# Polynomial-sketch attention followed by a ReGLU FFN: shared PSUM banks, attention released evenly over FFN units, and finer TensorE and ScalarE pieces

## The chip, the cores and the metric

The kernel runs on one core of one Trainium2 chip. The metric is the device time of one execution in microseconds (us). Before the change the median of three runs is 133.13 us (132.45 to 133.69). Five engines work beside each other, each through a queue of its own in order: TensorE (PE; its weight loads are listed as PEld), VectorE (DVE), ScalarE (ACT), GpSimd (POOL) and SyncE (SP, which here only issues DMAs). The PSUM memory, into which TensorE writes, has eight banks of 128 x 512 fp32.

## The reference

```python
def _attn_ref(q, k, v, S1, S2):             # q, k, v: (4, 4, 1088, 32); S1, S2: (8, 32)
    def phi(x):
        a = np.einsum('rd,bhsd->bhsr', S1, x)
        b = np.einsum('rd,bhsd->bhsr', S2, x)
        return np.einsum('bhsi,bhsj->bhsij', a, b).reshape(*x.shape[:-1], r * r)
    q_p, k_p = (phi(q), phi(k))
    kv = np.einsum('bhsf,bhsd->bhfd', k_p, v)
    z = np.sum(k_p, axis=2)
    num = np.einsum('bhsf,bhfd->bhsd', q_p, kv)
    den = np.einsum('bhsf,bhf->bhs', q_p, z)[..., None] + 1e-06
    return (num / den).astype(np.float32)

def _moe_ref(x, w_gate, w_val, w_out):      # x: (4352, 128), d_ff = 1536
    gate = np.maximum(x @ w_gate, 0.0)
    val = x @ w_val
    return (gate * val @ w_out).astype(np.float32)
```

The attention output, with its heads side by side, is the FFN's `x`: 4 batches x 1088 positions, 128 channels. All inputs and the output are fp32 in device memory.

## The kernel before

**The FFN.** It is cut into 102 units, in the order of ten groups of positions. A group is a pair of a batch and a first block of 128 positions. Batch 0 has three groups, of 256, 256 and 512 positions (units 0 to 5, 6 to 11 and 12 to 23). Batches 1 to 3 have two groups of 512 positions each, 12 units a group. The last group, of 256, holds the 64 last positions of all four batches (units 96 to 101). A unit takes 128 hidden channels for 512 positions, or 256 channels for 256 positions. Its steps are `gate` (L458, TensorE into a PSUM bank), `relu` (L464, ScalarE, PSUM to `g_sb`), `val` (L470, TensorE), `prod` (L475, VectorE, `g_sb` times the PSUM of `val`, into `ht`) and `out` (L485, four TensorE products that accumulate into the group's output bank over the group's units). After the last unit of a group, `store` (L493) copies the output bank to `o_sb` on ScalarE and SyncE sends it out (L496).

**Attention, keys.** Class `K` does one batch: `t1` transposes the keys (L249, VectorE, `kt`), `ab` multiplies them by the sketches in fp32 (L257, TensorE), `t2` transposes back (L267, `abk`), `phi` forms the outer products (L205, `kp`, mostly GpSimd), `kv` (L283) and `kv_rest` (L295) multiply by the values, `z` (L308) and `z_rest` (L318) sum the features in fp32, `zdiag` (L324) and `w` (L340) and `wfill` (L345) fold z into the matrix `wst` that queries are multiplied by, and `kvcopy` (L330) copies the product to `kv16` on ScalarE. Class `Rest` does the first of these for the 64 last positions.

**Attention, queries.** Class `Q` does one group: `t1` (L368, `qt`), `ab` (L378, TensorE, fp32), `t2` (L386, `abq`), `bw_` (L390), `den` (L396, L398), `an` (L403), `phi` (L205, `qp`), `tr` (L415, TensorE transposes), `tre` (L421, ScalarE, PSUM to `pt`), `num` (L432, TensorE) and `x` (L438, ScalarE, into `xT`). A group's first `gate` needs its `xT`. `phi` runs on GpSimd for all groups but the first, `bw_` and `an` from batch 1 on.

**Loads.** At the start come the sketches, batch 0 and, on GpSimd's queue, the weights. The keys and queries of batches 1 to 3 are loaded on SyncE's queue by `load_kq`, each behind a one-element ScalarE copy that waits for the weights (L715, L717). The values are loaded on GpSimd's queue (L90), in line with GpSimd's products.

**The order.** Every step is an `Op` with an engine, a planned duration, what it depends on, a level, a gate and the buffers that it holds. The planner `plan` runs when the program is built: it takes, step after step, the operation that its clock says can start first, and writes it to its engine's queue. A higher level goes ahead of a lower one on the same engine if it is ready within a slack. An operation with a gate isn't considered before the FFN unit of that number has its `gate` in the queue. The keys of batches 2 and 3 have gate "40 units before their first unit", the queries "20 units before". So the order of each queue is fixed in the program, and on the chip an engine waits at each instruction until its inputs and its buffer are there. A load of values counts for 0.9 us in the plan, the time of its issue. Where the planner sees a gap on TensorE early in the program, it fills it with products of zeros (`warm`, L158).

**PSUM.** The eight banks are four pools: two for gate products (`g_ps`), three for value products (`v_ps`), one for the output (`o_ps`, also the target of `warm`) and two for attention (`m_ps`). Batch 0's attention may use any but the output's.

## Time and profile before

| | |
|---|---|
| median of three runs | 133.13 us (132.45 to 133.69) |
| the profiled execution | 134.5 us, of which the span from the first to the last instruction is 132.8 us |
| mean granted TensorE clock | 0.954 of full speed |
| busy in the span | PE 119.1 us, DVE 95.3, ACT 80.8, POOL 47.8 |
| moved by DMA | 9.28 MB |

The profile is one execution. Times in it are in us from the start of the span. A row of the timeline has the start, the length, the engine, the line, what is written from what, the shapes and a count; a bracket gives the idle time of the engine ahead of it and what ended that. A row of the chain of waits has the start, the length on the chain and what ran. Product times are stretched: products follow each other in a pipeline, so that the distance between starts is what one costs, and a busy PE is not a PE at its peak. The granted clock is the share of full speed that TensorE had.

### The profile page before, as it was taken

How to read it: one execution, taken by the hardware profiler on the slowest of the kernel's cores; microseconds unless marked ns; L12 is line 12 of the kernel's file. 1: busy time of each engine (PE TensorE's matmuls, PEld its weight loads, DVE VectorE, ACT ScalarE, POOL GpSimd, SP SyncE). 2: the span in 40 equal slices, each digit the busy share in tenths (PEclk: the TensorE clock that was granted, in tenths of full speed). 3: DMA queues.
4: the chain of work that ended last, by engine and by line, in shares of the span. 5: the costliest groups of instructions: out<-in, count | busy, mean ns of one | idle time of the engine just before them, and what ended most of it. 6: DMA issues, size and time to landing. Idle time of an engine off the chain costs nothing.

```text
span 132.8 us, 2928 instructions
## 1 busy us (share of the span) xinstructions
PE 119.1 (90%) x1104; PEld 77.6 (58%) x1104; DVE 95.3 (72%) x198; ACT 80.8 (61%) x158; POOL 47.8 (36%) x62
## 2 busy tenths in 40 slices
...
GB/s 54 292 166 186 178 355 38 307 349 22 17 0 39 12 94 60 0 0 17 67 0 0 31 52 2 0 27 59 0 32 47 7 12 67 0 14 70 0 35 84
DMA packets 9521, 9.28 MB, mean 70 GB/s; under 512 B 3364, under 2 KB 7844, under 8 KB 9508
## 3 DMA queue, kind: packets, MB, share of 16 engines
...
q8 instruction: 8, 0.13, 0.4%
...
## 4 chain that ended last, share of the span: by engine, by line
PE 64%; DMA 14%; ACT 6%; DVE 6%; POOL 4%; issue 4%; POOLq 0%; DVEq 0%; ACTq 0%
PE o_ps L485 15%; PE g_ps L458 14%; PE v_ps L470 13%; DMA wv<-in_moe_w_val_dram 6%; PE m_ps L257 6%; ACT g_sb L464 5%; PE m_ps L378 5%; DMA k_sb<-in_k_dram 5%; DMA v_sb<-in_v_dram 3%; PE m_ps L308 3%; PE m_ps L415 2%; PE m_ps L432 2%; DVE abq L386 2%; DVE ht L475 2%; PE m_ps L318 2%
## 5 line engine op out<-in xcount | busy, mean ns | idle before, releaser
L475 DVE TENSOR_TENSOR ht<-g_sb,v_ps 128x512 f16<-128x512 f16 x102 | 64.1, 673 | 10.1 <-ACT g_sb L464 6.2
L464 ACT ACTIVATE g_sb<-g_ps 128x512 f16<-128x512 f32 x102 | 58.2, 599 | 15.8 <-PE g_ps L458 10.6
L458 PE MATMUL g_ps<-xT,wg 128*128 128x512 f16 (+1 forms) x120 | 37.6, 349 | 2.4 <-ACT g_sb L464 0.9
L485 PEld LDWEIGHTS <-ht 128*128 128x128 f16 x408 | 27.8, 99 | 19.3 <-DVE ht L475 11.2
L470 PE MATMUL v_ps<-xT,wv 128*128 128x512 f16 (+1 forms) x120 | 38.1, 354 | 0.0
L485 PE MATMUL o_ps<-wo,ht 128*128 128x128 f16 x408 | 37.3, 222 | 0.5 <-DVE ht L475 0.5
L390 POOL TENSOR_TENSOR bw<-abq 128x128 f32<-128x128 f32 (+1 forms) x7 | 3.0, 431 | 44.0 <-DVE abq L386 43.9
L205 POOL TENSOR_TENSOR kp<-abk 128x512 f16<-128x512 f32 x14 | 14.6, 1066 | 11.3 <-DVE abk L267 6.5
L205 POOL TENSOR_TENSOR qp<-an,abq 128x1024 f16<-128x1024 f32 (+1 forms) x9 | 15.8, 1754 | 4.5 <-DVE an L403 4.1
L458 PEld LDWEIGHTS <-wg 128*128 128x128 f16 x120 | 11.5, 99 | 7.0 <-issue 3.7
L470 PEld LDWEIGHTS <-wv 128*128 128x128 f16 x120 | 11.6, 99 | 4.3 <-issue 2.5
L421 ACT COPY pt<-m_ps 128x1024 f16<-128x1024 f16 (+1 forms) x10 | 8.8, 883 | 7.2 <-PE m_ps L415 6.9
L330 ACT ACTIVATE kv<-m_ps 64x64 f16<-64x64 f32 x16 | 3.5, 218 | 14.5 <-PE m_ps L295 7.9
L257 PE MATMUL m_ps<-kt,sk 128*128 128x512 f32 (+1 forms) x20 | 9.5, 613 | 2.1 <-DVE kt L249 2.1
L378 PE MATMUL m_ps<-qt,wst 128*128 128x512 f32 (+2 forms) x24 | 9.1, 482 | 0.0
L386 DVE STREAM_TRANSPOSE abq<-m_ps 128x512 f32<-128x512 f32 (+1 forms) x9 | 5.9, 656 | 4.0 <-PE m_ps L378 3.8
L158 PE MATMUL o_ps<-zero 128*128 128x128 f16 x87 | 7.5, 254 | 1.1 <-DVE maskw L145 1.1
L249 DVE STREAM_TRANSPOSE kt<-k_sb 128x512 f32<-128x512 f32 x8 | 5.4, 689 | 4.0 <-DMA k_sb<-in_k_dram 4.0
L438 ACT CAST xT<-m_ps 128x512 f16<-128x512 f32 (+1 forms) x10 | 5.2, 521 | 5.0 <-PE m_ps L432 4.9
L158 PEld LDWEIGHTS <-zero 128*128 128x128 f16 x87 | 6.6, 117 | 2.3 <-DVE maskw L145 1.1
L257 PEld LDWEIGHTS m_ps<-kt,sk 128*128 128x128 f32 x20 | 4.0, 216 | 5.4 <-DVE kt L249 3.1
L283 PE MATMUL m_ps<-v_sb,kp 128*128 128x64 f16 x64 | 3.5, 193 | 3.6 <-DMA v_sb<-in_v_dram 2.9
...
## 6 DMA issues: line engine op xcount, KB each, us to landing
...
```

Of the source, the lines that this page charges most:

```text
L158: nc.tensor.matmul(ps[:, 0:128], zero, zero, start=True, stop=True)
L205: eng.tensor_tensor(out=dst.rearrange("s x (i j) -> s x i j", i=R), in0=a_src[:, :, :, None].to_broadcast([dst.shape[0], n, R, R]), in1=ab ...
L249: nc.vector.transpose(self.kt[:, :, 2 * pr:2 * pr + 2], k_sb[self.b][:, 2 * pr:2 * pr + 2].rearrange("p h (c d) -> p c h d", d=D))
L257: nc.tensor.matmul(ps[:, 0:GC * n * 32].rearrange("p (c x) -> p c x", c=GC), sk[:, hf].rearrange("p a b f -> p (a b f)"), self.kt[:, hf * ...
L378: nc.tensor.matmul(self.ps[:, i * w:(i + 1) * w], wst[:, b].rearrange("p h f -> p (h f)"), self.qt.rearrange("p x t -> p (x t)")[:, i * w: ...
L386: nc.vector.transpose(self.absb.rearrange("p x f -> p (x f)"), self.ps[:, 0:n * 128])
L421: nc.scalar.copy(out=self.pt, in_=self.ps)
L458: nc.tensor.matmul(g_ps[:, y * W:(y + 1) * W], wg[:, j], xT[:, self.col:self.col + W], start=True, stop=True)
L464: nc.scalar.activation(out=self.g_sb, in_=self.g_ps, func=ACTF.Relu)
L470: nc.tensor.matmul(self.v_ps[:, y * W:(y + 1) * W], wv[:, j], xT[:, self.col:self.col + W], start=True, stop=True)
L475: nc.vector.tensor_tensor(out=self.ht, in0=self.g_sb, in1=self.v_ps, op=ALU.mult)
L485: nc.tensor.matmul(o[:, s], self.ht[:, y * W + x * 128:y * W + (x + 1) * 128], wo[:, j], start=(j == 0 and s == 0), stop=(j == NJ - 1), sk ...
```

## The change

PSUM: the four pools become eight pools of one bank each. The planner chooses for each product the bank that it expects to be free first, of banks 0 to 6, and of 7 and 6 for a group's output. In the plan at most two gate products, four value products and two outputs are open at once. `z` of batches 1 to 3 gets a bank of its own; before it shared that of `kv`.

Release: `spread` gives the steps of the keys and of a group's queries each a gate of its own, which rises evenly with their planned cost (GpSimd's counted half): the keys of a batch from 35 to 25 units before their first unit, the queries of a group from 20 to 8. Attention of batches 1 to 3 has level 0, as FFN units have. Where two operations can start at the same planned time, the higher level and then the one that has been ready longer goes first.

Pieces: `ab` of batches 1 to 3 is planned as four pieces instead of one, `kv` as four instead of two, `z` as four instead of one; TensorE's columns are the same in all. `tre` of a 512-position group is two copies of 128x512 instead of one of 128x1024. `zdiag`, `w` and `wfill` don't wait for `kv_rest` any more.

Loads: `load_kq` becomes `load_k` and `load_rest_q`, apart, each with a gate: the queries of batch 1 come after unit 0 has its gate product, the keys of batches 2 and 3 after units 4 and 20, their queries after units 10 and 24. The rest of the keys and values, on SyncE's queue, goes with the queries of batch 1.

```diff
-    ps_g = ctx.enter_context(tc.tile_pool(name="ps_g", bufs=2, space=bass.MemoryType.PSUM))
-    ps_v = ctx.enter_context(tc.tile_pool(name="ps_v", bufs=3, space=bass.MemoryType.PSUM))
-    ps_o = ctx.enter_context(tc.tile_pool(name="ps_o", bufs=1, space=bass.MemoryType.PSUM))
-    ps_m = ctx.enter_context(tc.tile_pool(name="ps_m", bufs=2, space=bass.MemoryType.PSUM))
...
+    ps = [ctx.enter_context(tc.tile_pool(name=f"ps{i}", bufs=1, space=bass.MemoryType.PSUM))
+          for i in range(8)]
+
+    def bank(i):
+        return ps[i].tile([128, 512], FP32, name=f"bank{i}")
...
+        def ab(self, x, h0, n, lo, w, hf):
+
+            if x is not None:
+                self.ps[h0] = bank(x)
+            nc.tensor.matmul(
+                self.ps[h0][:, lo * n * 32:(lo + w) * n * 32].rearrange("p (c x) -> p c x", c=w),
+                sk[:, hf].rearrange("p a b f -> p (a b f)"),
+                self.kt[:, hf * GC + lo:hf * GC + lo + w, h0:h0 + n].rearrange(
+                    "p c h t -> p c (h t)"),
+                start=(hf == 0), stop=(hf == 1), skip_group_check=True)
...
+        def kv(self, x, c):
+
+            if c == 0:
                 self.m = bank(x)
...
+        def z(self, x, c):
+            if c == 0:
                 self.zps = bank(x)[:, 0:64]
...
-        def tre(self, eng):
-            self.pt = a_kp.tile([128, 2 * self.n, 128], FP16, name="pt")
-            nc.scalar.copy(out=self.pt, in_=self.ps)
+        def tre(self, lo, hi):
+            if lo == 0:
+                self.pt = a_kp.tile([128, 2 * self.n, 128], FP16, name="pt")
+            nc.scalar.copy(out=self.pt[:, lo:hi], in_=self.ps[:, lo:hi])
...
             if self.first:
-                F.o = ps_o.tile([128, 4, DM], FP32, name="o_ps")
-            o = F.o
+                F.o[self.b, self.c0] = bank(x).rearrange("p (s m) -> p s m", s=4)
+            o = F.o[self.b, self.c0]
...
-    SLACK = (0.0, 250.0, 60.0, 0.0)
-    BUFS = {"m": 2, "g": 2, "v": 3, "o": 1, "kt": 3, "qt": 3, "abk": 2, "abq": 2, "kp": 2,
+    SLACK = (0.0, 60.0, 60.0, 0.0)
+    BUFS = {**dict.fromkeys(range(8), 1), "g": 2, "v": 4, "o": 2, "kt": 3, "qt": 3, "abk": 2, "abq": 2, "kp": 2,
...
-            t0 = max([clock[o.eng], o.at] + [after(d, o) for d in o.deps])
+            ready = max([o.at, begun[max(0, -int(-o.gate // 1))] if o.gate > -1 else 0.0]
+                        + [after(d, o) for d in o.deps])
+            t0 = max(clock[o.eng], ready)
...
-            for o, t, x in can:
-                if best and t >= best[1]:
+            for o, t, x, ready in can:
+                key = t, -o.level, ready
+                if best and key >= best[0]:
                     continue
-                best = o, t, x
-            o, t, x = best
+                best = key, o, t, x
+            _, o, t, x = best
...
                 unit = o.unit
+                begun.append(t)
...
+    K0, KA, KB, QA, QB = 2, 35, 25, 20, 8
...
+        lv, lo_lv = (2, 1) if first else (0, 0)
...
+            new = []
+            for lo in range(0, GC, w):
+                for hf in range(2):
+                    new.append(op("PE", 55 * n * w, kb.ab, h0, n, lo, w, hf,
+                                  deps=(*t1s[h0 // 2:(h0 + n) // 2], sk_fill, *abs_[-1:], *behind),
+                                  bank=(None,) if new else banks, level=lv, **kw))
+                    abs_.append(new[-1])
+            t2 = op("DVE", 60 + 140 * n, kb.t2, h0, n, deps=(abs_[-1], *t2s[-1:]), level=lv, **kw)
+            hold("bank", new[0], t2)
...
-        for i in range(2):
-            kvs.append(op("PE", 620, kb.kv, 2 * i,
-                          deps=(*phis[2 * i:2 * i + 2], *kvs, *loaded), level=1, **kw))
...
-        else:
-            z = op("PE", 1300, lambda: kb.z(None), deps=tuple(kvs), level=1, **kw)
-        zr = op("PE", 500, kb.z_rest, x, deps=(z, rest_t2), level=lv, **kw)
-        kr_ = op("PE", 300, kb.kv_rest, x, vt, deps=(kvs[1], rest_phi, zr), level=1, **kw)
-        hold("abk", t2s[0], z)
-        hold("kp", t2s[0], kvs[1])
-        zd = op("DVE", 200, kb.zdiag, deps=(zr, *(() if first else (kr_,))), level=lv, **kw)
...
+        zs = []
+        for c in range(GC):
+            zs.append(op("PE", 330, kb.z, c, deps=(*t2s, *zs[-1:]), level=lv,
+                         bank=(None,) if zs else banks, **kw))
+        zs.append(op("PE", 500, kb.z_rest, x, deps=(zs[-1], rest_t2), level=lv, **kw))
+        zd = op("DVE", 200, kb.zdiag, deps=(zs[-1],), level=lv, **kw)
+        hold("bank", zs[0], zd)
+        wp = op("PE", 420, kb.w, deps=(zd, s1_copy), bank=banks, level=lv, **kw)
+        wf = op("DVE", 200, kb.wfill, deps=(wp, f0), level=lv, **kw)
+        hold("bank", wp, wf)
+        hold("zd", zd, wp)
+        for c in range(GC):
+            kvs.append(op("PE", 280, kb.kv, c, bank=(None,) if kvs else banks,
+                          deps=(*phis[c // 2 * 2:c // 2 * 2 + 2], *kvs[-1:], *loaded), level=lo_lv, **kw))
+        kvs.append(op("PE", 300, kb.kv_rest, x, vt, deps=(kvs[-1], rest_phi), level=lo_lv, **kw))
+        hold("abk", t2s[0], kvs[-2])
...
-        w = op("PE", 420, kb.w, deps=(zd, s1_copy), bank=banks, level=lv, **kw)
-        wf = op("DVE", 200, kb.wfill, deps=(w, f0), level=lv, **kw)
-        hold("bank", w, wf)
-        hold("zd", zd, w)
-        if not first:
-            cps[-1].deps += (zd,)
...
-        tre = op("ACT", 150 + 225 * c, qk.tre, nc.scalar, deps=(tr,), **kw)
+        tres = []
+        for lo in range(0, 2 * c, 4):
+            tres.append(op("ACT", 600, qk.tre, lo, lo + 4, deps=(tr, *tres[-1:]), **kw))
...
-                g = op("PE", 222, u.gate, deps=(x, *gs[-1:]), at=10500.0)
+                g = op("PE", 222, u.gate, deps=(x, *gs[-1:]), at=10500.0, bank=range(7))
...
+                hold("bank", g, rl)
+                v = op("PE", 222, u.val, deps=(x, *vs[-1:]), at=13500.0, bank=range(7))
...
+                outs.append(op("PE", 228, u.out, deps=(p, *outs[-1:]), at=16500.0,
+                               bank=None if outs else (7, 6)))
...
+    def spread(first, u0, u1):
+
+        new = ops[first:]
+        cost = [o.ns * (0.5 if o.eng == "POOL" else 1.0) for o in new]
+        done = 0.0
+        for o, c in zip(new, cost):
+            o.gate = u0 + (u1 - u0) * done / sum(cost)
+            done += c
+
+    def load_k(b):
         nc.scalar.copy(out=k_sb[b][0:1, 0, 0:1], in_=wv[0:1, 0, 0:1])
         load_main(nc.sync, k_sb[b], k, b)
+
+    def load_rest_q(b):
         nc.scalar.copy(out=q_sb[b][0:1, 0, 0:1], in_=wv[0:1, 0, 0:1])
...
-    rest = (*add_rest(128, kr, 0.0, 1, 4), vr)
-    cast = op("ACT", 400, lambda: nc.scalar.copy(out=vr, in_=vr32), gate=4)
+    rest = (*add_rest(128, kr, 26000.0, 0, 7), vr)
+    cast = op("ACT", 400, lambda: nc.scalar.copy(out=vr, in_=vr32), gate=9, at=29000.0)
...
-            op("ACT", 250, load_kq, b, at=13500.0 + 3000 * (b - 1))
-        kv, wf = add_k(b, rest if b else rest0, [(4300.0, 5300.0), (18000.0,) * 2, (0.0,) * 2, (0.0,) * 2][b],
-                       s - 40 if b > 1 else -1, any_bank if b < 1 else ("m",), lv,
+            op("ACT", 200, load_k, b, at=13500.0, gate=[0, -1, 4, 20][b])
+            op("ACT", 200, load_rest_q, b, gate=[0, 0, 10, 24][b])
...
+        if b:
+            spread(n0, max(K0, s - KA), max(K0 + 8, s - KB))
...
+                if b:
+                    spread(n0, start[grp] - QA, start[grp] - QB)
...
+    spread(n0, start[groups[-1]] - QA - 2, start[groups[-1]] - QB)
```

What this does to the queues is shown at three places. Names are those of the steps above; `bank`, `m_ps` and `g_ps` are PSUM, and the lines of the changed kernel differ by a few from those before.

VectorE at the start of the program, where batch 0's keys (`abk`, `kp`, `zd`, `wst`) and its first queries (`qt`, `abq`) alternate; before:

```order
L267 STREAM_TRANSPOSE abk<-m_ps 128x4x64
L368 STREAM_TRANSPOSE qt<-q_sb_104 128x256
L267 STREAM_TRANSPOSE abk<-m_ps 128x4x64
L232 STREAM_TRANSPOSE abr_208<-g_ps 32x256
L205 TENSOR_TENSOR kp<-abk 128x512 x2
L368 STREAM_TRANSPOSE qt<-q_sb_104 128x256
L324 TENSOR_TENSOR zd<-m_ps,maskz 128x64
L368 STREAM_TRANSPOSE qt<-q_sb_104 128x512
L345 TENSOR_TENSOR wst<-m_ps,maskw 128x4x8
L386 STREAM_TRANSPOSE abq<-m_ps 128x256
```

and now:

```order
L265 STREAM_TRANSPOSE abk<-bank_242 128x4x64
L362 STREAM_TRANSPOSE qt<-q_sb_116 128x256
L229 STREAM_TRANSPOSE abr_220<-bank_253 32x256
L265 STREAM_TRANSPOSE abk<-bank_248 128x4x64
L362 STREAM_TRANSPOSE qt<-q_sb_116 128x256
L362 STREAM_TRANSPOSE qt<-q_sb_116 128x512
L202 TENSOR_TENSOR kp<-abk 128x512 x2
L318 TENSOR_TENSOR zd<-bank_276,maskz 128x64
L339 TENSOR_TENSOR wst<-bank_296,maskw 128x4x8
L380 STREAM_TRANSPOSE abq<-bank_308 128x256
```

The second transpose of `abk` goes behind that of the rest (`abr`), and two transposes of queries, of 256 and 512 columns, go ahead of `kp`, `zd` and `wst`. On TensorE, `w` stands behind the first four products of `kv` now, and stood ahead of all of them before; the first `ab` of the queries stands behind twelve of the sixteen `kv` products, before behind eight, and two more `ab` stand ahead of `kv_rest`, before none.

VectorE where the first FFN products (`ht`) stand, beside the keys of batch 1 (`kt`, `abk`), its first queries (`qt` from `q_sb`) and the rest (`ktr`, `abr`); before:

```order
L403 TENSOR_TENSOR an<-abq,rd 128x128
L249 STREAM_TRANSPOSE kt<-k_sb_101 128x8x64 x2
L475 TENSOR_TENSOR ht<-g_sb,v_ps 128x512 x3
L267 STREAM_TRANSPOSE abk<-m_ps 128x512
L222 STREAM_TRANSPOSE ktr<-kr 128x256
L368 STREAM_TRANSPOSE qt<-q_sb_105 128x512
L232 STREAM_TRANSPOSE abr_210<-m_ps 128x256
L475 TENSOR_TENSOR ht<-g_sb,v_ps 128x512 x4
```

and now:

```order
L397 TENSOR_TENSOR an<-abq,rd 128x128
L471 TENSOR_TENSOR ht<-g_sb,bank_428 128x512
L471 TENSOR_TENSOR ht<-g_sb,bank_437 128x512
L246 STREAM_TRANSPOSE kt<-k_sb_113 128x8x64 x2
L362 STREAM_TRANSPOSE qt<-q_sb_117 128x512
L471 TENSOR_TENSOR ht<-g_sb,bank_440 128x512
L471 TENSOR_TENSOR ht<-g_sb,bank_445 128x512
L471 TENSOR_TENSOR ht<-g_sb,bank_466 128x512
L471 TENSOR_TENSOR ht<-g_sb,bank_476 128x512
L219 STREAM_TRANSPOSE ktr<-kr 128x256
L471 TENSOR_TENSOR ht<-g_sb,bank_523 128x512
L265 STREAM_TRANSPOSE abk<-bank_550 128x512
```

Two products go ahead of `kt` and four more ahead of `abk`; the transpose of batch 1's queries goes ahead of the third product. On TensorE, batch 1's `ab` stands behind four units' outputs, in four pieces with FFN products between; before it stood whole, ahead of the first output.

GpSimd's queue with the loads of the values of batches 2 and 3 (`v_sb`), among the key products (`kp`, `kpr`) and the queries' steps (`bw`, `an`, `qp`) of batches 1 and 2; before:

```order
L390 TENSOR_TENSOR bw_155<-abq 128x16x8
L205 TENSOR_TENSOR kp<-abk 128x512
L403 TENSOR_TENSOR an<-abq,rd 128x128
L205 TENSOR_TENSOR kp<-abk 128x512
L205 TENSOR_TENSOR qp<-an,abq 128x1024
L390 TENSOR_TENSOR bw_154<-abq 128x16x8
L90 DMA v_sb_110<-in_v_dram 128x4x256
L403 TENSOR_TENSOR an<-abq,rd 128x128
L205 TENSOR_TENSOR qp<-an,abq 128x1024
L90 DMA v_sb_111<-in_v_dram 128x4x256
```

and now:

```order
L202 TENSOR_TENSOR kp<-abk 128x512 x4
L202 TENSOR_TENSOR kpr_223<-abr_222 128x512
L87 DMA v_sb_122<-in_v_dram 128x4x256
L384 TENSOR_TENSOR bw_167<-abq 128x16x8
L397 TENSOR_TENSOR an<-abq,rd 128x128
L202 TENSOR_TENSOR qp<-an,abq 128x1024
L384 TENSOR_TENSOR bw_166<-abq 128x16x8
L87 DMA v_sb_123<-in_v_dram 128x4x256
L202 TENSOR_TENSOR kp<-abk 128x512 x4
L397 TENSOR_TENSOR an<-abq,rd 128x128
```

The load for batch 2 goes ahead of batch 1's `bw` instead of behind the second `bw`, and all four `kp` of batch 2 come after both loads instead of before them. On TensorE, the first `kv` of batch 2 stands behind unit 22's output; before it stood behind unit 21's gate product.

143 lines of the change are left out of this document (58 added, 85 removed).

## The prediction, made before the changed kernel was run

> **What bounds the kernel now.** I read the page first: TensorE is busy for most of the span, more than any other engine (the table above), and more than half of the chain that ended last is TensorE's. Where it stands still or runs slowly is read from the busy time by stretch (columns: stretch, length, busy time and count of PE, PEld, DVE, ACT and POOL, granted clock, DMA share, GB/s):
>
> ```profile
> 17.40:25.30 7.90, 5.84 (x33) 3.08 (x33) 4.04 (x9) 3.22 (x10) 1.95 (x1) 0.78 0.62 196
> ...
> 45.40:55.50 10.10, 7.16 (x56) 5.39 (x56) 2.19 (x5) 3.01 (x9) 2.61 (x2) 0.67 0.44 52
> ...
> 95.80:106.60 10.80, 10.37 (x95) 5.63 (x95) 9.13 (x17) 8.81 (x16) 2.81 (x3) 1.00 0.10 27
> ...
> 117.60:125.80 8.20, 8.20 (x82) 5.78 (x80) 8.15 (x13) 7.47 (x14) 0.00 (x0) 1.00 0.12 32
> ```
>
> The first two stretches have a lowered clock and little work done; the third is one group of twelve units late in the run; in the last, TensorE never pauses. TensorE's timeline shows the edges of the two bad places:
>
> ```profile
> 17.43 0.38 PE L458 MATMUL g_ps<-xT,wg 128*128 128x256 f16 x2 [0.48 <-ACT xT L438]
> ...
> 21.75 3.56 PE L257 MATMUL m_ps<-kt,sk 128*128 128x512 f32 x4 [1.91 <-DVE kt L249]
> 25.15 0.61 PE L415 MATMUL m_ps<-ident,qp 128*128 128x128 f16 x8
> ...
> 48.34 0.63 PE L283 MATMUL m_ps<-v_sb,kp 128*128 128x64 f16 x16 [2.95 <-DMA v_sb<-in_v_dram]
> ...
> 55.51 0.69 PE L415 MATMUL m_ps<-ident,qp 128*128 128x128 f16 x8
> ...
> 128.20 0.40 PE L485 MATMUL o_ps<-wo,ht 128*128 128x128 f16 x4 [0.25 <-DVE ht L475]
> ```
>
> So I sum TensorE's work from the first gate product (17.43) to the last output (end 128.6), and count what is lost beside it. The chain of waits has the price of each piece at full clock (start, length on the chain, what):
>
> ```profile
> 62.27 0.93 PE m_ps L378 x2
> ...
> 66.22 1.98 PE m_ps L257 x4
> ...
> 68.65 0.45 PE m_ps L415 x8
> ...
> 70.40 0.33 PE m_ps L432 x8
> ...
> 71.72 0.23 PE m_ps L283 x8
> ...
> 73.71 0.92 PE m_ps L308 x8
> 74.63 0.56 PE m_ps L318 x4
> ...
> 76.08 0.42 PE m_ps L340 x4
> ...
> 109.73 0.84 PE m_ps L378 x8
> ...
> 119.31 0.22 PE o_ps L485 x4
> ...
> 122.58 0.22 PE o_ps L485 x4
> ```
>
> The last two rows are outputs five units apart: (122.58 - 119.31) / 5 = 0.654 us a unit, 66.7 for 102. A batch of keys is 1.98 + 2 x 0.23 + 0.92 + 0.56 + 0.42, and about 0.2 for `kv_rest` (an estimate from L283's price): 4.5, for three batches 13.6. A group of queries is 0.93 + 0.45 + 0.33 = 1.71, for six 10.3. The last group is 0.84 and half of 0.45 + 0.33, and some overhead for its many small products: 1.4. For batch 0's two later groups (half of `tr` and `num`, and the whole) I take 1.3, for the rest's `ab` 0.4. Sum: 93.7 us.
>
> From 17.43 to 128.6 are 111.2 us, so 17.5 are lost. The first place costs 1.91 idle and 3.40 (21.75 to 25.15) for `ab` instead of 1.98: 3.3. The second costs 2.95 idle, and 7.17 us (48.34 to 55.51) for work that at full clock is 0.46 + 0.33 + 0.92 + 0.56 + 0.2 + 3 x 0.22 + 4 x 0.22 = 4.0: together 6.1. The other 8.1 are in small pieces over 100 us.
>
> **The second place goes.** There TensorE waited for the values of batch 2, whose load stood on GpSimd behind a `bw`:
>
> ```profile
> 43.60 0.45 POOL L390 TENSOR_TENSOR bw<-abq 128x128 f32<-128x128 f32 x1 [0.28 <-DVE abq L386]
> 43.99 0.80 POOL L90 DMA_DIRECT2D v_sb<-in_v_dram  x1
> ```
>
> From issue to TensorE's start are 4.35 us. In the changed queue the load stands behind batch 1's key products alone, which end by about 33 us if `abk` is there by 27.8 (five products of about 1.06, of which two took 2.09 in the row of the start below); it would land by 38. The first `kv` of batch 2 stands behind unit 22's output, which comes after 45 by the sum below. So 6.1 becomes 0. The load of batch 3 moves ahead of batch 2's `kp`, with some 20 units in hand. If GpSimd came 8 us later than this, the wait would be back.
>
> **The start gets later.** These rows are of VectorE, GpSimd and TensorE in batch 0's chain:
>
> ```profile
> 8.50 1.24 DVE L205 TENSOR_TENSOR kp<-abk 128x512 f16<-128x512 f32 x2
> ...
> 10.34 0.70 DVE L368 STREAM_TRANSPOSE qt<-q_sb 128x512 f32<-128x512 f32 x1
> ...
> 12.65 0.45 DVE L386 STREAM_TRANSPOSE abq<-m_ps 128x256 f32<-128x256 f32 x1 [1.24 <-PE m_ps L378]
> ```
> ```profile
> 10.63 2.09 POOL L205 TENSOR_TENSOR kp<-abk 128x512 f16<-128x512 f32 x2
> ```
> ```profile
> 13.27 0.70 PE L378 MATMUL g_ps<-qt,wst 128*128 128x256 f32 x2
> 13.81 1.39 PE L158 MATMUL o_ps<-zero 128*128 128x128 f16 x22
> 15.04 0.39 PE L415 MATMUL m_ps<-ident,qp 128*128 128x128 f16 x4
> 15.26 1.08 PE L378 MATMUL m_ps<-qt,wst 128*128 128x512 f32 x2
> ```
>
> Two `qt` (0.70, and about 0.4 for the smaller one, an estimate from its columns) now precede `kp`, so VectorE ends `zd` and `wst` about 0.7 later, and the queries' first `ab` needs the second GpSimd `kp` as well (end 12.72 before, about 0.3 earlier now, since `abr` goes ahead): `abq` starts at about 13.4 instead of 12.65. Then the other two `ab` (0.6 + 0.9) precede `kv_rest`, and 20 products of zeros (1.39 for 22) precede the first `tr`: about 16.3 instead of 15.04, of which 16 further zeros hide nothing. The first gate product comes 0.3 to 1.1 late; I take 0.9, since each piece has a row: 18.3.
>
> **The first place shrinks.** Before, VectorE's queue stood at `kt` until batch 1's keys had landed, and all products stood behind it:
>
> ```profile
> 20.39 1.30 DVE L249 STREAM_TRANSPOSE kt<-k_sb 128x512 f32<-128x512 f32 x2 [1.92 <-DMA k_sb<-in_k_dram]
> ```
> ```profile
> 14.20 6.10 DMA k_sb<-in_k_dram
> ```
> ```profile
> 22.09 0.38 SPq L90 DMA_DIRECT2D k_sb<-in_k_dram  x1
> ```
> ```profile
> 24.00:24.50 0.50, 0.50 (x2) 0.02 (x1) 0.00 (x0) 0.00 (x0) 0.00 (x0) 0.50 0.91 315
> ```
> ```profile
> L464 ACT ACTIVATE g_sb<-g_ps 128x512 f16<-128x512 f32 x102 | 58.2, 599 | 15.8 <-PE g_ps L458 10.6
> ```
>
> Now two products precede `kt`, and the keys have the DMA queue to themselves until the first `xT`, so I expect no wait for them at about 20.1 (18.3, a relu of 0.6 and its waits, two products at 8.15 / 13 = 0.63). But batch 1's queries are issued only after that `xT`, at about 18.4, and their `qt` stands ahead of the third product, at 21.4. How long this load takes has two bounds: the loads issued from 22.09 on move at 315 GB/s from 24.0 on, so 544 KB (557,000 bytes) take 1.8 after a start of 1.9, landing at 22.1; the keys of batch 1, beside other loads, took 6.1, which would be 24.5. The first is nearer, since nothing large runs beside it: a wait of about 0.7. TensorE has 5.1 us of work ahead of batch 1's `ab` (six gate, eight value products and four outputs at 0.22, and 1.3 for batch 0's queries). ScalarE's queue (five relus at 0.6, three copies and two `xT` at about 0.5, together some 6 us) lets it get there at about 24.3: 0.9 lost instead of 3.3 (bounds 0.5 and 5).
>
> Here a rule is weighed. The rows are the pause of 1.91 us above and the clock of 0.50 behind it, at which four products took 3.56 us that take 1.98 at full clock. The Trainium skill (TensorE: Matmul & The Clock Gate, Part 1) says that the clock halves only after an idle window of about 3.4 us, and is full again after as long a busy one. The trace disagrees on the first: a pause of 1.91 was enough. By that rule a wait of 3 us for the queries would leave the clock alone; by the row it costs about 1.6 (half of 3.3) on top, and so I price it.
>
> **The small losses.** Of the 8.1, about 1.2 is the end (the last unit's relu, product and output one behind the other), which stays. About 1.2 are lost at each boundary between groups late in the run (10.80 in the third stretch, less the 9.6 of work, below):
>
> ```profile
> 97.36 0.69 DVE L475 TENSOR_TENSOR ht<-g_sb,v_ps 128x512 f16<-128x512 f16 x1 [1.20 <-ACT g_sb L464]
> ```
> ```profile
> 94.37 1.01 ACT L421 COPY pt<-m_ps 128x1024 f16<-128x1024 f16 x1
> 95.28 0.60 ACT L493 ACTIVATE o_sb<-o_ps 128x512 f32<-128x512 f32 x1
> 96.24 0.58 ACT L438 CAST xT<-m_ps 128x512 f16<-128x512 f32 x1 [0.36 <-PE m_ps L432]
> ```
>
> ScalarE runs three copies in a row and no relu, VectorE drains, TensorE then waits. Split and spread copies, a second output bank and a fourth value bank can take part of this away, but TensorE's own work (12 x 0.654 + 1.71 = 9.6 of the 10.80 us of the third stretch) leaves little to win: between 0 and 4.6, and I take 2, leaving 6.1. It could also grow by 1: each `tre` now pays ScalarE's fixed time twice. The finer `ab`, `kv` and `z` have the same columns, so I take them at zero: TensorE goes from piece to piece without a wait in the chain's rows. SyncE's queue has three loads behind stores now, each some 20 units ahead of its use: zero too.
>
> **Sum.** 18.3 + 93.7 + 0.9 + 6.1 + 4.2 (from 128.6 to the span's end, the last store) = 123.2 us span. The execution shown took 134.5, 1.7 above its span: 124.9. It lies 1.4 above the median of the runs shown, and so I take 1.4 off: 123.5 us, 7% less than 133.13.
>
> **The rivals.**
> 1. More of the small losses goes: 3.5 left instead of 6.1, 120.9, with a start only 0.3 late about 120. For it: the last stretch above, where TensorE has no pause at all. Against: in the third stretch VectorE is busy for 9.13 us too, and could set the pace soon. Chance 0.13.
> 2. The queries of batch 1 land at 24.5 and VectorE stands with all products behind: 2.4 us more (24.5 less 22.1) and a slow clock for 3.3 us (1.6), 127.5, and up to 129 if the start or the small losses are 1.5 worse as well. Chance 0.13.
> 3. The lead is lost again: attention, spread between units at level 0, brings `xT` late, and each of seven boundaries costs 1.2 more than now: 8.4, about 132, no change. Between units 23 and 24 TensorE's queue now holds no gate product for five outputs, two pieces of `z`, `z_rest`, `num`, four `kv` and `w`, so the place exists; but the other boundaries have `xT` five units ahead or more. Chance 0.06.
> 4. Slower: TensorE now walks through eight single banks, each handed back by ScalarE or VectorE, and if it pauses often enough the clock falls again and again. One fall costs about 1.6 (3.3 us at half clock, as at 21.75), so six falls take the gain of 9.6 away and the seventh makes it slower; a fall in every other 3.4 us of 105 us, 15 of them, gives 148, ten give 140. Against: in the third stretch the clock is 1.00 although TensorE stood still for 0.43 of 10.80, and the changed plan has as many banks for FFN products as before (five) at the worst. Chance 0.08. The Trainium skill (TensorE: Matmul & The Clock Gate, A second HAM failure mode: psum-queue depth-cycling) tells of such a kernel; the trace of before shows none of it.
>
> **The numbers.** The forecast has 0.60. A measurement of this kernel can tell about 1% from no change. Faster by over 1% is forecast, rivals 1 and 2: 0.86, of which I keep 0.84, for what none of these names; within 1% 0.06; slower 0.10. The range is from 119.5 (rival 1) to 129 (rival 2), and leaves out rivals 3 and 4 and a little more at each end.
>
> **What would show it.** Right: no wait for `v_sb`; a first gate product near 18.3; unit 24's gate product near 49 us (18.3 + 15.7 for 24 units + 1.3 + 0.4 + 4.5 and 4.0 for two batches of keys + 2.6 for queries + 0.9 + some 1.5 lost); in the last stretch 0.654 us a unit. Wrong: a wait for `q_sb` on VectorE of over 1 us, a clock below 1.00 between 18 and 115 us, or more than 6 us of TensorE's time lost after unit 24.

## The result, and the profile after

The changed kernel takes 125.35 us (median of 4 runs, 125.03 to 126.52) against 133.36 us (4 runs, 132.45 to 133.69) of the kernel before beside it: a ratio of 0.9425, with an interval of 0.9359 to 0.9491. Executions over 1.5% above the fastest of the same kernel are left out of the ratios, here and below. The prediction said 123.5 us, 119.5 to 129. The total came out close. Two of its terms did not: the start was 3.8 us worse than predicted, and the small losses 3.4 us better.

The page of the profiled execution (126.52 us; span, busy time, granted clock in 40 slices, and the engines' shares of the chain that ended last):

```profile
span 123.9 us, 2888 instructions
...
PE 114.9 (93%) x1117; PEld 80.6 (65%) x1117; DVE 97.3 (78%) x198; ACT 81.3 (66%) x165; POOL 46.8 (38%) x62
...
PEclk9999559999999999999999999999999999999995
...
PE 74%; DVE 11%; DMA 5%; ACT 4%; issue 2%; SPq 1%; ACTq 0%
```

TensorE has less busy time than before, in a span 8.9 us shorter. The one low clock inside the work now lies at about 12 to 19 us; the two of before, at 21 to 25 and at 48 to 56, are gone.

TensorE's timeline has the edges of what follows (first gate product, batch 1's first `ab`, the place where the values of batch 2 were late before, unit 24's gate product, the last output):

```profile
22.11 0.38 PE L454 MATMUL bank<-xT,wg 128*128 128x256 f16 x2 [0.48 <-ACT xT L433]
...
28.37 1.08 PE L254 MATMUL bank<-kt,sk 128*128 128x256 f32 x4
...
50.69 0.29 PE L280 MATMUL bank<-v_sb,kp 128*128 128x64 f16 x4
...
51.58 0.38 PE L454 MATMUL bank<-xT,wg 128*128 128x512 f16 x1
...
119.30 0.40 PE L481 MATMUL bank<-wo,ht 128*128 128x128 f16 x4 [0.23 <-DVE ht L471]
```

From the start of the first gate product to that of the last output are 97.2 us; before, they were 128.20 - 17.43 = 110.8. So 13.6 us were won behind the start and 4.7 lost at it. The two spans differ by 8.9 us and the medians by 8.0, so about 1 us of the 13.6 may belong to the one profiled execution of the kernel before. This stretch is the measure of all experiments below, since it leaves the start out.

**The start.** VectorE, then GpSimd, then TensorE in batch 0's chain:

```profile
9.00 0.98 DVE L362 STREAM_TRANSPOSE qt<-q_sb 128x256 f32<-128x256 f32 x2
9.92 3.17 DVE L202 TENSOR_TENSOR kp<-abk 128x512 f16<-128x512 f32 x2
13.01 0.21 DVE L318 TENSOR_TENSOR zd<-bank,maskz 128x64 f32<-128x64 f32 x1
```
```profile
8.82 1.06 POOL L202 TENSOR_TENSOR kpr<-abr 32x512 f16<-32x512 f32 x1 [1.35 <-DVE abr L229]
9.85 2.08 POOL L202 TENSOR_TENSOR kp<-abk 128x512 f16<-128x512 f32 x2
```
```profile
12.54 0.39 PE L280 MATMUL bank<-v_sb,kp 128*128 128x64 f16 x4 [1.76 <-DVE kp L202]
...
15.87 2.91 PE L372 MATMUL bank<-qt,wst 128*128 128x256 f32 x4
```
```profile
L202 DVE TENSOR_TENSOR kp<-abk x2: 680/1620/2561, 9.9 to 12.4; 128x512 f16<-128x512 f32 x2
```

VectorE's two `kp` took 1.24 us before, from 8.50 on. Now they start at 9.92, while GpSimd makes its own, and take 3.17: 2561 ns for one and 680 ns for the other (the last row: least, median, greatest). GpSimd's two end at 11.9 and VectorE's first some 0.5 later, so VectorE seems to have stood until GpSimd was done. TensorE stood still for 1.76 us; its clock fell to half at about 12.1, within that pause, and stayed there until 18.9.

### The profile page after: what moved, and what is told of

Read it like the earlier page. It is cut to its first block, busy times and chain, and to the rows that moved or that the text cites. A ratio compares the mean times of both kernels' runs of the same rounds, so it can differ in the third digit from the quotient of the medians.

```text
span 123.9 us, 2888 instructions
## 1 busy us (share of the span) xinstructions
PE 114.9 (93%) x1117; PEld 80.6 (65%) x1117; DVE 97.3 (78%) x198; ACT 81.3 (66%) x165; POOL 46.8 (38%) x62
## 4 chain that ended last, share of the span: by engine, by line
PE 74%; DVE 11%; DMA 5%; ACT 4%; issue 2%; SPq 1%; ACTq 0%
PE bank L454 16%; PE bank L481 16%; PE bank L466 15%; PE bank L372 8%; DVE ht L471 8%; PE bank L254 5%; DMA q_sb<-in_q_dram 5%; PE bank L409 3%; ACT g_sb L460 2%; PE bank L427 2%; PE bank L302 2%; PE bank L280 2%; PE bank L334 2%; PE bank L155 2%; PE bank L312 1%
## 5 line engine op out<-in xcount | busy, mean ns | idle before, releaser
L471 DVE TENSOR_TENSOR ht<-g_sb,bank 128x512 f16<-128x512 f16 x102 | 65.7, 676 | 11.3 <-ACT g_sb L460 5.3
L460 ACT ACTIVATE g_sb<-bank 128x512 f16<-128x512 f32 x102 | 60.0, 602 | 15.7 <-PE bank L454 13.7
L481 PE MATMUL bank<-wo,ht 128*128 128x128 f16 x408 | 39.3, 219 | 0.6 <-DVE ht L471 0.6
L454 PE MATMUL bank<-xT,wg 128*128 128x512 f16 (+1 forms) x120 | 38.7, 347 | 0.6 <-ACT xT L433 0.5
L466 PE MATMUL bank<-xT,wv 128*128 128x512 f16 (+1 forms) x120 | 38.3, 347 | 0.4 <-DVE ht L471 0.4
L372 PE MATMUL bank<-qt,wst 128*128 128x512 f32 (+2 forms) x26 | 11.4, 553 | 0.0
L416 ACT COPY pt<-bank 128x512 f16<-128x512 f16 x17 | 10.0, 596 | 1.4 <-PE bank L409 1.4
L254 PE MATMUL bank<-kt,sk 128*128 128x256 f32 x32 | 9.6, 396 | 0.0
L380 DVE STREAM_TRANSPOSE abq<-bank 128x512 f32<-128x512 f32 (+1 forms) x10 | 6.3, 633 | 2.9 <-PE bank L372 2.9
L155 PE MATMUL bank<-zero 128*128 128x128 f16 x88 | 7.5, 256 | 1.1 <-DVE maskw L142 1.1
(73 smaller groups left out, 98.7 us busy)
## 6 DMA issues: line engine op xcount, KB each, us to landing
wo<-in_moe_w_out_dram POOLq DMA_DIRECT2D x1, 384.0 KB, 10.2
```

Of the source, the lines that this page charges most:

```text
L155: nc.tensor.matmul(w_ps[:, 0:128], zero, zero, start=True, stop=True)
L254: nc.tensor.matmul(self.ps[h0][:, lo * n * 32:(lo + w) * n * 32].rearrange("p (c x) -> p c x", c=w), sk[:, hf].rearrange("p a b f -> p (a ...
L372: nc.tensor.matmul(self.ps[:, i * w:(i + 1) * w], wst[:, b].rearrange("p h f -> p (h f)"), self.qt.rearrange("p x t -> p (x t)")[:, i * w: ...
L380: nc.vector.transpose(self.absb.rearrange("p x f -> p (x f)"), self.ps[:, 0:n * 128])
L416: nc.scalar.copy(out=self.pt[:, lo:hi], in_=self.ps[:, lo:hi])
L454: nc.tensor.matmul(g_ps[:, y * W:(y + 1) * W], wg[:, j], xT[:, self.col:self.col + W], start=True, stop=True)
```

## The experiments

**Summary.** "Stretch" is the time between the starts of the first gate product and of the last output, from TensorE's timeline of each profile. Ratios are to the kernel before, beside which each run was timed; the medians of all its executions there were 133.4, 134.1 and 133.1, and the ratios stand nearer to 1 than these medians do. The profiled executions of e1_start, e2_vload, e6_fill and e12_best had a slow beginning (told of under e6_fill), which makes their first gate product about 2 us later than it would be otherwise. For after_again, e5_kpfirst, e6_fill and e7_tre there is no ratio.

| kernel | median us (range of 4) | ratio (interval) | first gate | last output | stretch |
|---|---|---|---|---|---|
| before | | | 17.43 | 128.20 | 110.8 |
| changed | 125.35 (125.03 to 126.52) | 0.9425 (0.9359 to 0.9491) | 22.11 | 119.30 | 97.2 |
| e1_start | 127.00 (125.44 to 127.28) | 0.9638 (0.9468 to 0.9809) | 23.27 | 120.64 | 97.4 |
| e2_vload | 128.82 (127.88 to 129.09) | 0.9788 (0.9652 to 0.9925) | 19.90 | 122.78 | 102.9 |
| e3_banks | 128.61 (128.09 to 129.17) | 0.9800 (0.9616 to 0.9983) | 22.02 | 121.78 | 99.8 |
| e4_nospread | 128.76 (128.08 to 129.30) | 0.9794 (0.9649 to 0.9939) | 22.05 | 121.74 | 99.7 |
| after_again | 126.04 (125.44 to 126.90) | | 22.03 | 119.39 | 97.4 |
| e5_kpfirst | 124.04 (121.68 to 124.69) | | 17.76 | 118.25 | 100.5 |
| e6_fill | 125.64 (122.84 to 126.40) | | 22.62 | 119.99 | 97.4 |
| e7_tre | 131.36 (130.78 to 131.60) | | 21.79 | 125.48 | 103.7 |
| e9_tre_order | 126.58 (125.96 to 127.71) | 0.9702 (0.9537 to 0.9868) | 20.53 | 119.22 | 98.7 |
| e10_banks_order | 126.04 (124.28 to 126.52) | 0.9549 (0.9325 to 0.9774) | 22.07 | 119.31 | 97.2 |
| e11_kp_ahead | 134.30 (133.75 to 135.13) | 1.0270 (1.0167 to 1.0374) | 20.91 | 127.42 | 106.5 |
| e12_best | 121.58 (121.35 to 123.17) | 0.9319 (0.9181 to 0.9456) | 19.68 | 116.83 | 97.2 |

### The late values alone: e2_vload

```diff
-            lv = (op("POOL", 900, load_main, nc.gpsimd, v_sb[b], v, b, gate=[0, -1, 10, 20][b],
-                     at=13000.0), cast)
+            lv = (op("POOL", 900, load_main, nc.gpsimd, v_sb[b], v, b, gate=[0, -1, 1, 20][b],
+                     at=13000.0, level=2 if b == 2 else 0), cast)
```

> The kernel before with one thing changed: batch 2's value load is issued on GpSimd some twenty units earlier, ahead of batch 1's products; all else keeps the plan of before. Theory A (the prediction's step): the wait of 2.95 us for v_sb and the half clock behind it cost 6.1 us, and nothing else is late in their place: 133.4 becomes about 127.3, with a clock of 1.00 between 45 and 56 us. Theory B: the load was only the last of several late things, so the key products or the copies behind it set the same time: 131 to 133. Theory C: the load, now early, runs beside batch 1's loads and makes the first place longer: the second place gains 6 and the first loses 1 to 3, 128 to 131.

The ratio of 0.979 is about 2.8 us less (1.0 to 4.6 by its interval). TensorE's timeline has batch 1's `ab`, and the stretches (columns as in the table of stretches of the prediction) the place of the old wait:

```profile
22.36 1.98 PE L257 MATMUL m_ps<-kt,sk 128*128 128x512 f32 x4
```
```profile
40.00:45.00 5.00, 4.63 (x57) 3.71 (x55) 2.62 (x5) 2.85 (x8) 2.35 (x2) 1.00 0.11 31
45.00:50.00 5.00, 4.63 (x32) 1.98 (x30) 3.30 (x8) 3.80 (x7) 2.13 (x4) 1.00 0.08 5
```

No wait for `v_sb`, and the clock stays at 1.00. The stretch is 7.9 us shorter than before; 3.3 of that is the first place, which vanished in this profile because its first gate product came 2.5 us later, after a slow beginning, and the keys had landed by then (`ab` in 1.98, no pause ahead of it). That leaves about 4.6 for the late values, where the prediction had 6.1: in their place TensorE loses some 0.7 at 40 to 50 us, and other small amounts. Theory A holds in kind; in size it is 4.6 by the two profiles and 2.8 by the ratio, both under its 6.1.

### PSUM banks, even release, split copies: one undone at a time

e3_banks gives each kind of product its own banks again (gates 0 and 1, values 2 to 4, outputs 7; 5 and 6 for attention of batches 1 to 3 and of batch 0's third group). e4_nospread leaves out the even release:

```diff
         if b:
-            spread(n0, max(K0, s - KA), max(K0 + 8, s - KB))
+            pass
...
                 if b:
-                    spread(n0, start[grp] - QA, start[grp] - QB)
+                    pass
...
-    spread(n0, start[groups[-1]] - QA - 2, start[groups[-1]] - QB)
```

e7_tre makes one copy of two:

```diff
-        for lo in range(0, 2 * c, 4):
-            tres.append(op("ACT", 600, qk.tre, lo, lo + 4, deps=(tr, *tres[-1:]), **kw))
+        tres.append(op("ACT", 150 + 220 * c, qk.tre, 0, 2 * c, deps=(tr,), **kw))
```

> The changed kernel with its PSUM banks divided as before: gates two banks, values three, outputs one, attention two (batch 0's attention may still use any). All the rest of the change stays. Theory A: the sharing of banks, the second output bank and the fourth value bank are what made the small losses after 18 us smaller than the prediction's 6.1: they return, 125.4 becomes 128 to 130, with TensorE waiting for a bank at each group boundary. Theory B: the even release and the finer pieces did it, the banks hardly matter: within 1% of 125.4.

> The changed kernel without the even release: the steps of a batch's keys and of a group's queries are all released at once, 40 and 20 units ahead of their use, as before; banks and finer pieces stay as changed. Theory A: the even release keeps ScalarE and VectorE from getting several attention steps in a row, and without it each of the seven boundaries costs about 0.5 to 1 more: 128 to 132. Theory B: serving by readiness and shared banks do it already: within 1% of 125.4. Theory C: released at once, attention is done early and the end is better: about 124.

> The changed kernel with one part undone: ScalarE copies the turned query features of a group in one piece (1.0 us for a group of four) instead of two (0.6 each). Theory A: two pieces keep the relu from being held up a whole microsecond; in one piece TensorE waits at the boundaries again, 0.2 to 0.5 each: 126.5 to 129. Theory B: the split costs ScalarE 0.2 us a group and gains nothing: 124.5 to 125.5.

All three are slower than the changed kernel, and theory A was named for each. But the timelines of TensorE show that their pauses lie at one and the same place, ahead of the first gate product of unit 24. They are 2.7 us in e3_banks, which lost 2.6, and 1.4 in e4_nospread, which lost 2.5. e3_banks:

```profile
52.41 0.62 PE L409 MATMUL bank<-ident,qp 128*128 128x128 f16 x8 [0.87 <-POOL qp L202]
54.20 0.40 PE L427 MATMUL bank<-pt,kv 128*32 128x256 f16 x8 [1.16 <-ACT pt L416]
55.28 0.38 PE L454 MATMUL bank<-xT,wg 128*128 128x512 f16 x1 [0.69 <-ACT xT L433]
```

e4_nospread and, below it, e7_tre:

```profile
54.78 0.38 PE L454 MATMUL bank<-xT,wg 128*128 128x512 f16 x1 [1.07 <-ACT xT L433]
```
```profile
52.70 0.84 PE L409 MATMUL bank<-ident,qp 128*128 128x128 f16 x8 [1.21 <-POOL qp L202]
54.65 0.62 PE L427 MATMUL bank<-pt,kv 128*32 128x256 f16 x8 [1.10 <-ACT pt L416]
55.95 0.58 PE L454 MATMUL bank<-xT,wg 128*128 128x512 f16 x1 [0.68 <-ACT xT L433]
```

The changed kernel has this gate product at 51.58 without a pause. In two of the three TensorE first waits for `qp` of GpSimd, so GpSimd's timeline is the next view. The changed kernel, then e3_banks:

```profile
44.05 0.41 POOL L397 TENSOR_TENSOR an<-abq,rd 128x128 f32<-128x128 f32 x1 [0.85 <-DVE rd L392]
44.53 1.96 POOL L202 TENSOR_TENSOR qp<-an,abq 128x1024 f16<-128x1024 f32 x1
...
47.67 4.14 POOL L202 TENSOR_TENSOR kp<-abk 128x512 f16<-128x512 f32 x4
```
```profile
45.54 4.14 POOL L202 TENSOR_TENSOR kp<-abk 128x512 f16<-128x512 f32 x4
...
50.42 1.94 POOL L202 TENSOR_TENSOR qp<-an,abq 128x1024 f16<-128x1024 f32 x1
```

The changed kernel makes batch 1's first `qp` and then batch 2's four `kp`. In e3_banks (and in e4_nospread and e7_tre, where the four start at 41.46 and 45.02) the `kp` go first: products for units from 48 on stand ahead of the one that unit 24 waits for. The planner's clock had come out a little different with each undone part, and that was enough to swap them. That gave a new theory: the order of one `qp` and four `kp` on GpSimd is what the three runs lost, and not the banks or the copies themselves. The even release can't be told from the order by these runs, since what it changes is the order; e4_nospread, where TensorE doesn't wait for `qp`, was not run with the order put back.

### The order alone: e9_tre_order, e10_banks_order, e11_kp_ahead

Into e7_tre and e3_banks one dependence is put that makes batch 2's `kp` on GpSimd wait for that `qp` (e9_tre_order and e10_banks_order):

```diff
-                               nc.vector if dve else nc.gpsimd, c, 2, deps=tuple(t2s), level=lo_lv, **kw))
+                               nc.vector if dve else nc.gpsimd, c, 2,
+                               deps=(*t2s, *((made[1, 0, GC][1],) if b == 2 else ())), level=lo_lv, **kw))
...
+        made[grp] = an, phis[-1]
```

Into the changed kernel goes the opposite one (e11_kp_ahead):

```diff
+        if b == 2:
+            made[1, 0, GC][0].deps += (phis[-1],)
...
+        made[grp] = an, phis[-1]
```

> e7_tre (ScalarE's copy in one piece) with one order put back as the changed kernel has it: GpSimd makes qp of batch 1's first query group ahead of batch 2's four kp. Theory A: in e7_tre the planner, given other copy times, put the four kp (4.1 us) ahead of that qp, so that unit 24's xT came 4 to 5 us late; the copy's form is not the cause, and with the order back the time is 125.5 to 127. Theory B: the one long copy itself holds ScalarE up at the boundaries: 129 to 131, as e7_tre's 131.4.

> e3_banks (PSUM banks divided as before) with the same order put back on GpSimd. Theory A: the order of that one qp was what e3_banks lost; the division of the banks itself costs under 1 us: 125.5 to 126.5. Theory B: the banks themselves are worth it: 128 to 129, as e3_banks's 128.6.

> The changed kernel with the opposite order alone: GpSimd makes batch 2's four kp ahead of an and qp of batch 1's first query group; banks, split copies and even release stay. Theory A: unit 24's xT comes some 4 us late, TensorE drains at 50 to 55 us as in the three runs that undid one part each, and the time is 128 to 131. Theory B: with shared banks and split copies TensorE finds other work: within 1% of 126.

With the order put back, the divided banks cost nothing that can be seen: a stretch of 97.2, as the changed kernel's. The copy in one piece costs about 1.5 us of the 6.5 that e7_tre lost (98.7 against 103.7 and 97.2). TensorE's row at unit 24 of e9_tre_order and of e10_banks_order:

```profile
50.95 0.38 PE L454 MATMUL bank<-xT,wg 128*128 128x512 f16 x1 [0.41 <-ACT xT L433]
```
```profile
52.77 0.38 PE L454 MATMUL bank<-xT,wg 128*128 128x512 f16 x1 [0.69 <-ACT xT L433]
```

The opposite order, with banks, copies and release as changed, makes the kernel slower than before the change, 134.3 us. On GpSimd nothing but this `an` and `qp` changes place; the other queues are what the planner then makes of it, here and in the two runs above. TensorE's rows, and the stretches behind:

```profile
54.28 1.03 PE L409 MATMUL bank<-ident,qp 128*128 128x128 f16 x8 [3.97 <-POOL qp L202]
56.48 0.62 PE L427 MATMUL bank<-pt,kv 128*32 128x256 f16 x8 [1.16 <-ACT pt L416]
57.78 0.58 PE L454 MATMUL bank<-xT,wg 128*128 128x512 f16 x1 [0.68 <-ACT xT L433]
```
```profile
50.00:55.00 5.00, 1.03 (x15) 0.89 (x12) 0.00 (x0) 0.87 (x4) 4.22 (x4) 0.65 0.19 48
55.00:60.00 5.00, 3.16 (x23) 1.77 (x22) 0.25 (x1) 2.92 (x6) 0.00 (x0) 0.50 0.26 81
```

The pauses are 5.8 us (3.97 + 1.16 + 0.68), the clock is at half from 51.5 to 61.7 us, and the stretch is 9.3 us longer than the changed kernel's. It was more than theory A's 128 to 131; the expectation left the clock out. So one swap on an engine that is busy for 38% of the span costs as much as the whole change won (8.0 us). That shows what a wrong order there costs, and not that the order is where the gain over the kernel before came from.

### The start: e1_start, e5_kpfirst, e6_fill, after_again

e1_start delays, in the plan, the second and third query transposes of batch 0, so that VectorE's `kp` stand ahead of them:

```diff
-                x, ab = add_q(grp, len(xs), (kv,), (wf,), 7000.0, -1 if g0 else start[grp] - 20,
+                x, ab = add_q(grp, len(xs), (kv,), (wf,), {6: 9500.0, 12: 10300.0}.get(start[grp], 7000.0), -1 if g0 else start[grp] - 20,
```

> The changed kernel with one order put back: in batch 0's chain VectorE makes its two kp ahead of the second and third qt, as the kernel before did (the assumed landing of these queries in the planner is 9500 and 10300 instead of 7000). Theory A: the first gate product comes at 22.1 instead of 17.4 because VectorE's kp started while GpSimd's kp ran and took 2.56 us for the first of two; with VectorE first it takes about 1.3 for both, the pause of 1.76 on TensorE becomes about 1.1 or less, the clock stays at 1.00, and the first gate product comes at about 18.5. If the rest follows one for one, 125.35 becomes about 121.8. Theory B: the start is later because of the order on TensorE itself (w behind the first values, the queries' ab ahead of kv_rest), which is left as it is: the gate product stays near 21 to 22 and the time within 1%. Theory C: the gate product comes early but the lead is given back at the first wait for batch 1's keys or queries: about 125, since the executions of the changed kernel whose mean clock was 0.998 had spans only 0.4 us shorter than those at 0.962.

The gate product came at 23.27, or by estimate 21.4 without the slow beginning of this execution (1.9 less, as between e12_best and e5_kpfirst), and the time is 127.0: theory A fell in this form. VectorE's timeline, then GpSimd's:

```profile
11.04 3.67 DVE L202 TENSOR_TENSOR kp<-abk 128x512 f16<-128x512 f32 x2
```
```profile
10.45 1.05 POOL L202 TENSOR_TENSOR kpr<-abr 32x512 f16<-32x512 f32 x1 [3.00 <-DVE abr L229]
11.48 2.08 POOL L202 TENSOR_TENSOR kp<-abk 128x512 f16<-128x512 f32 x2
```

GpSimd's `kpr` had already begun when VectorE's `kp` came, as in the changed kernel; VectorE was slow again. What counts is not where VectorE's `kp` stand among the transposes but which engine begins first, and that goes back to `abr`, which the change put ahead of the second `abk`. e5_kpfirst keeps e1_start's edit and undoes that as well (and lets GpSimd's `kp` stand behind its `kpr`, as before):

```diff
-        t2 = op("DVE", 360, x.t2, deps=(ab,), **kw)
+        t2 = op("DVE", 360, x.t2, deps=(ab,), at=8600.0 if n == 32 else 0.0, **kw)
...
-                               nc.vector if dve else nc.gpsimd, c, 2, deps=tuple(t2s), level=lo_lv, **kw))
+                               nc.vector if dve else nc.gpsimd, c, 2,
+                               deps=(*t2s, *((rest_phi,) if first and hf else ())), level=lo_lv, **kw))
```

> The changed kernel with batch 0's start in the order of before where VectorE and GpSimd meet: the second abk ahead of abr, VectorE's two kp directly behind them and ahead of the later qt, GpSimd's two kp behind its kpr. w and the queries' ab then come ahead of the first values on TensorE by the planner's own choice; all from the first gate product on keeps its order. Theory A: who starts first decides; VectorE's two kp take 1.3 us instead of 3.2, and GpSimd's kpr 2.0 instead of 1.05; zd comes at about 10.5 instead of 13.0, no pause of TensorE reaches 1.7 us, and the first gate product comes at 18 to 19; the span falls by about 3 to 121, the time to about 122. Theory B: the pause and the half clock come anyway, since TensorE now waits for GpSimd's second kp (end near 13): gate product at 20 to 21, time about 124. Theory C: early gate products, but the first wait for batch 1's keys gives all back: 125.

VectorE, GpSimd and TensorE:

```profile
9.03 1.24 DVE L202 TENSOR_TENSOR kp<-abk 128x512 f16<-128x512 f32 x2
...
23.11 0.71 DVE L362 STREAM_TRANSPOSE qt<-q_sb 128x512 f32<-128x512 f32 x1 [1.81 <-DMA q_sb<-in_q_dram]
```
```profile
9.18 2.02 POOL L202 TENSOR_TENSOR kpr<-abr 32x512 f16<-32x512 f32 x1 [1.74 <-DVE abr L229]
```
```profile
17.76 0.38 PE L454 MATMUL bank<-xT,wg 128*128 128x256 f16 x2 [0.47 <-ACT xT L433]
...
24.45 0.58 PE L466 MATMUL bank<-xT,wv 128*128 128x256 f16 x2 [2.32 <-DVE ht L471]
```
```profile
25.00:30.00 5.00, 5.00 (x38) 3.63 (x36) 2.32 (x4) 1.87 (x4) 0.00 (x0) 0.71 0.34 106
```

Now VectorE begins first: its two `kp` take 1.24 us and GpSimd's `kpr` is the one that is stretched, 2.02 us. Of theory A all comes true up to the first gate product, 17.76. The run also brings `w` and the queries' `ab` forward on TensorE, and no run parts that from VectorE's order. Behind it theory C takes over in part: 3.3 us of the 4.3 are given back (a stretch of 100.5), since batch 1's queries, loaded only after the first `xT`, are now late, VectorE stands at their `qt` with the products behind it, and the clock falls in TensorE's pause of 2.32 us. The four executions spread from 121.68 to 124.69, and this profile is of one of 124.58; whether the fastest waited too isn't shown.

e12_best takes that wait away by loading the queries with the keys:

```diff
-            op("ACT", 200, load_rest_q, b, gate=[0, 0, 10, 24][b])
+            op("ACT", 200, load_rest_q, b, gate=[0, -1, 10, 24][b], at=13600.0)
```

> e5_kpfirst (the order of before where VectorE and GpSimd meet in batch 0) with one thing more: batch 1's query load is issued with its key load, at about 16 us, instead of after the first xT at about 18. Theory A: in e5_kpfirst the lead of 4.3 us at the first gate product was given back since VectorE stood 1.8 us at qt, waiting for this load, with three products behind it, and TensorE 2.3 us; with the load earlier the wait goes, and the time falls to 121 to 122.5. Theory B: the load, issued beside the key load and the weights, lands no earlier: 124. Theory C: it delays the keys or the first xT: 124 to 126.

121.58 us (ratio 0.9319, 0.9181 to 0.9456): theory A. It beats both kernels; its slowest run, 123.17, is below the fastest of the eight of the changed kernel, 125.03. In its profile no `qt` waits, TensorE's only pause there is the one that the changed kernel has too, and the stretch is back at 97.2. Over e5_kpfirst that is a gain in this profile's stretch and in the median, and none over that run's fastest execution (121.68 against 121.35):

```profile
19.68 0.38 PE L454 MATMUL bank<-xT,wg 128*128 128x256 f16 x2 [0.47 <-ACT xT L433]
24.44 0.38 PE L466 MATMUL bank<-xT,wv 128*128 128x256 f16 x2 [0.39 <-DVE ht L471]
```

That its first gate product came at 19.68 and not near 17.8 has to do with the very beginning, which differs between executions: the first six `ab` take 2.87 us here and 1.56 in e5_kpfirst. e6_fill puts products of zeros into the pause of 1.76 us:

```diff
             if c == 0:
                 self.m = bank(x)
+                if self.b == 0:
+                    warm(30)
```

> The changed kernel with 30 products of zeros (about 1.7 us at full speed) put on TensorE ahead of batch 0's first values, in the pause of 1.76 us; nothing else moves. Theory A: the pause is what halves the clock; filled, the clock stays at 1.00 and the work from 12.5 to 18.7 takes about 3 us less: gate product near 19.5, time 122 to 123, unless the start before it was slow. Theory B: the clock falls although TensorE has something to do: no change, 125 to 126.

> The changed kernel itself once more, beside the next runs on the same chip. Both theories: 125 to 126.5. It shows which of two starts it takes: the one of its profile so far (the keys' ab at full speed, 2.2 us for eight products from 5.8 on, later a pause of 1.76 us and half clock) or one with slow ab at the start, as e1_start and e2_vload showed (3.7 us for eight products).

after_again came out as the changed kernel had: 126.0 us, and its profile has half clock from 12.3 to 19.1 after a pause of 1.44 us. e6_fill, 125.6, can't be told from it, and its profiled execution had the other beginning. TensorE's timeline of after_again, then that of e6_fill and a stretch of it:

```profile
5.94 1.51 PE L254 MATMUL bank<-kt,sk 128*128 128x256 f32 x6
...
12.27 0.39 PE L280 MATMUL bank<-v_sb,kp 128*128 128x64 f16 x4 [1.44 <-DVE kp L202]
```
```profile
6.25 2.87 PE L254 MATMUL bank<-kt,sk 128*128 128x256 f32 x6
```
```profile
9.00:10.00 1.00, 1.00 (x3) 0.18 (x2) 0.08 (x1) 0.00 (x0) 0.00 (x0) 1.00 0.86 169
```

Six `ab` take 2.87 us in one and 1.51 in the other, so TensorE still ran at about half speed there, although the clock of that stretch is given as 1.00. In e6_fill all four executions had a mean clock of 0.987 or more, and those of after_again 0.962 to 0.976, which fits a pause that no longer halves the clock. But two executions of the changed kernel, without the zeros, had 0.998 and 0.999 at 125.28 and 125.03 us, so the clock can stay up without them and the time be about the same; they left no profile. A slow beginning doesn't settle it either: e1_start had one, and its clock still fell, at 16.4 us. The one execution of 122.84 us in e6_fill may be the fast beginning with the filled pause, but it left no profile. e6_fill stays inconclusive.

## Why the prediction was right, and where it was not

By its own sum (span 123.2): the first gate product 18.3, work 93.7, first place 0.9, second place 0, small losses 6.1, tail 4.2. Measured: 22.1, the same 93.7 (taken over as estimated; late outputs come 0.658 us apart, where it has 0.654), 1.2, 0, 2.7 and 4.2, together 123.9. That the span is off by only 0.7 us is luck: two terms that were mis-sized cancel. The median is off by 1.9, mostly through the 1.4 us taken off for the one execution of before: the spans of the changed kernel's other executions, 123.3 to 123.7, lie only 0.2 to 0.6 below the profiled one.

- **The second place goes: right.** The values' load no longer stands behind work that waits, the first `kv` of batch 2 comes at 50.69 without a pause, and the clock there is full. e2_vload shows it alone, at about 4.6 us by the stretches (2.8 by the ratio) rather than 6.1: some of what lay behind the wait was late anyway.
- **The start gets later: the step that failed.** It let two `qt` precede `kp` and put the first gate product 0.9 us later, with bounds of 0.3 and 1.1; it measured 4.7. The step moved instructions with their durations, and put at nothing what VectorE and GpSimd cost each other when they meet. The sign was in GpSimd's timeline of before, and the step didn't read it: there `kpr`, beside VectorE's `kp`, took 2.01 us, and the two products after it 2.09 together.

```profile
8.64 2.01 POOL L205 TENSOR_TENSOR kpr<-abr 32x512 f16<-32x512 f32 x1 [1.20 <-DVE abr L232]
```

  In its place the two `kp` took 3.17 us instead of 1.24, and with VectorE first the gate product comes at 17.76 (e5_kpfirst, which moves `w` and the queries' `ab` too). Part of the 4.7 is the clock, at half for 6.8 us in and behind the pause that the slow `kp` makes. In e9_tre_order and e11_kp_ahead, whose VectorE has the same order here, it was at half for 3.4 us, and the gate product came at 20.53 and 20.91.
- **The first place shrinks: right, partly for another reason.** From 22.11 to 28.37 are 6.3 us for 5.1 of work, 1.2 lost where 0.9 was said. (The step's own terms, 18 products at 0.22 and 1.3, add up to 5.3; with that it is 1.0.) The wait for the queries that the step priced at 0.7 didn't come, because the load was quicker. It is issued behind the first `xT`, at 22.17 here and at 17.82 in e5_kpfirst, and VectorE comes to their `qt` 3.4 and 3.5 us after that. Here the load had landed by then, with no DMA moving between 20 and 22 us; in e5_kpfirst it took 5.3 us, while 1.09 MB moved from 18 to 22 us, about twice its own size, and VectorE waited 1.81 us and the stretch lost 3.3. That is the second rival, which the failed step had hidden.
- **Small losses: mis-sized.** 6.1 predicted, 2.7 measured (97.2 of stretch and 0.4 for the last output, less 93.7 and 1.2). The first rival (3.5 left) came true in this, with a start that was worse than its own. From 60 to 115 us TensorE is busy for 54.84 us, 53.24 before. What of the change did this isn't settled: divided banks give nothing back (e10_banks_order), the copy in one piece about 1.5 us (e9_tre_order). The release, the order by readiness and the finer products were not tried apart with the order on GpSimd held.
- **The other rivals.** The third named the boundary between units 23 and 24, and that is where the change can be lost. Its mechanism, a late release, is not what was seen: the four `kp` on GpSimd are (e11_kp_ahead, 9.3 us). In the changed kernel itself the order is the good one, and unit 24's gate product comes at 51.58, 2.6 later than the 49 predicted, with a start 3.8 later. The fourth rival, a clock that falls again and again among single banks, didn't happen: the page's clock line has nothing below 9 from the seventh slice to the last but one.
- **The signs.** Of those of being right, no wait for `v_sb` came, and the late units at 0.658 us; the first gate product and unit 24's did not. Of those of being wrong one came, by the failed step: a clock below 1.00 until 18.9 us.
- **The weighed rule.** The Trainium skill (TensorE: Matmul & The Clock Gate, Part 1) asks for an idle window of about 3.4 us before the clock halves. The runs disagree on the idle window: the clock fell in a pause of 1.76 us in the changed kernel, behind one of 1.44 in after_again, and behind one of 1.21 in e7_tre. They agree on its length: in all these profiles a spell of half clock that is over before the span ends lasts 3.4, 6.8 or (e11_kp_ahead) 10.2 us, and in the kernel before the falls, at 21.5, 48.8 and 130.8 us, are 8 and 24 times 3.41 us apart. So the clock seems to be set anew once in 3.41 us, from a stretch that need not be idle throughout.
